# A retention layer with a Mish feed-forward on one core: a weight cast shared by two engines, GpSimd's casts ahead of a load, a state product put later, and a PSUM tile from another pool

## The chip, the cores and the metric

The kernel runs on one core of a Trainium2 chip. The core's engines run side by side: TensorE (PE) multiplies matrices, VectorE (DVE), ScalarE (ACT) and GpSimd (POOL) work elementwise, SyncE (SP) issues DMAs, and GpSimd and ScalarE can issue DMAs too. The metric is the device time of one execution in microseconds, as the median of several runs. Lower is better.

## The reference

For each batch and head a state of 64 x 64 is decayed and updated token by token; the query reads it. The result, laid out as 3072 tokens of 512 features, goes through two matrix products with an activation between them.

```python
batch, n_heads, seq, head_dim = (4, 8, 768, 64)      # q, k, v; float32
gamma = 1.0 - 2.0 ** (-5.0 - np.arange(H))
for t in range(S):
    state = gamma * state + einsum('bhd,bhe->bhde', k[:, :, t], v[:, :, t])
    y[:, :, t] = einsum('bhd,bhde->bhe', q[:, :, t], state) / sqrt(64)
x = y.transpose(0, 2, 1, 3).reshape(3072, 512)
h = x @ w_in                                          # 512 x 2048
out = (h * tanh(softplus(h))) @ w_out                 # 2048 x 512, float32
```

## The kernel before

**Chunks and blocks.** The 24 chunks of 128 tokens (six in each batch) are worked through in blocks: block 0 has four chunks, blocks 1 to 10 two each. The retention is done by chunk: `scores` multiplies k and q of one chunk (into a PSUM tile `at`), `mask` makes them causal on VectorE (`am`), `y_two` gathers a block's output `y_ps` from the masked scores and the carried state, and ScalarE copies it to `xt`, the input of the feed-forward. `state_sum` and `state_decay` carry the state on; at the first chunk of a batch `state_sum` is a single product from PSUM (L467).

**The feed-forward.** Block 0 is done plainly: `g1` makes the 16 row blocks of the hidden layer (L560) with a Mish on ScalarE behind each (L576), and `first_g2` multiplies by the output weights (L1038, L1097). Each later block is two matrices of 2 x 2 parts multiplied with seven products instead of eight. `g1_seven` is the first matrix product (L685, for the two halves g = 0 and 1 of the hidden layer), with snapshots of single products (`hsnap`, L695 on ScalarE, one on VectorE at L693), additions on VectorE (`hsum`, L705) and Mish on ScalarE (L700). `seven` is the second (L798), with sums of the hidden parts `gsum` made by VectorE (L618, L619, L764, L768), snapshots (L807) and additions (L820). The differences of weights that the seven products need are made once: `wsum` (L643) and `tmat` (L595 to L598).

**Order.** The order of the instructions on each engine is the order in which the code calls them; no scheduler moves them. An engine works through its list in order and stops at an instruction whose operands or buffers are not ready, with everything that stands behind it. Work is woven in at named steps: in block 0 `plan` says what follows which row block, in later blocks `steps_of_first` (block 1) and `steps_of` (blocks 2 to 10) give lists that `step(name)` runs.

**Output weights.** They come in four slices of 4 x 512 columns. `cast_wout(s, on_act)` makes slice s float16: VectorE casts the first part (L198), ScalarE the last `on_act` of its four parts, two at a time (L200). Slice 1 was cast whole by VectorE, behind the sums `g_sum(1)` and `g_sum(2)`. In `first_g2` the products stand in the order slice 0, the sum with `tmat`, slice 1, slice 2, and so on; between them chunk 5 (counted from 1; index CPB = 4) and the next are turned on TensorE (`turn`, L427 and L429).

**GpSimd.** It casts q (`cast_q`, L376) and v (`cast_v`, L393) and issues the DMAs of k (`bring_k`, L388, two for each chunk from the seventh on; L385 before). `gate` is a copy of one column (L401) that makes GpSimd wait for a VectorE result, here for a `tmat`. From the seventh chunk on SyncE turns q and k by DMA (`turn_by_dma`, L405), once k has landed and q is cast.

**PSUM.** Two pools share it: `mmps` with four tiles (tag `mm`) for products, `atps` with two larger tiles (tag `at`) for scores, outputs `y_ps`, states and half of the `h_ps` tiles. A tile taken from a pool waits for the last reader of the tile whose place it takes.

Of the kernel before, what the change touches and what calls it, by code (L numbers as in the profile page):

```python
# [10 lines left out]
FP32 = mybir.dt.float32  # L11
# [5 lines left out]
def kernel(  # L17
# [11 lines left out]
    d_model, d_ff = moe_w_in.shape  # L29
    P = 128  # L30
# [5 lines left out]
    CPB = TB // C  # L36
# [62 lines left out]
    for c in range(2):  # L99
        t = tri_first[c * HB:(c + 1) * HB]  # L100
# [272 lines left out]
    def cast_q(g):  # L373
        if g < NCK:
            f = qs.rearrange("p (x j) -> p x j", x=2).unsqueeze(3)
            nc.gpsimd.tensor_tensor(  # L376
                by_head(g, room16(g)[0]), by_head(0, loaded[g][0]),
                f.broadcast_to((P, 2, HP, D)), op=ALU.mult)

    def bring_k(g):  # L380
        if g < NCK:
            b, c = divmod(g, NCH)
            src = k[b, :, c * C:(c + 1) * C].rearrange("h p d -> p h d")
            if g < NCH:
                nc.gpsimd.dma_start(room16(g)[1], src)  # L385
                return
            for x in range(2):
                nc.gpsimd.dma_start(  # L388
                    room16(g)[1][:, x::2], src[:, HP * x:HP * x + HP])
# [13 lines left out]
    def turn_by_dma(g):  # L403
        qkt = qktp.tile([P, H, C], FP16, name="qkt", bufs=4)
        nc.sync.dma_start_transpose(qkt, cast[g][3].rearrange("p a h d -> p (a h d)"))  # L405
        qkts[g] = (qkt[:, :HP], qkt[:, HP:])
# [243 lines left out]
    def x_sums(blk):  # L650
# [5 lines left out]
        nc.vector.tensor_tensor(t[:, 2], b[1][1], b[0][1], op=sub)  # L656
        nc.vector.tensor_tensor(t[:, 3], b[1][0], t[:, 1], op=sub)

    def g1_seven(blk, steps):
        n = NBP // 2  # L660
        gt = gtiles[blk, 0] = gp.tile([P, NFB, 2 * P], FP16, name="g", tag="g")
        for fb in range(NFB):
            gts[blk, fb] = gt[:, fb]
        both = atps.tile([P, 2, FPS, P], FP32, name="h_ps", tag="at")
        pb, px, pe, px1 = [
            mmps.tile([P, FPS, P], FP32, name="h_ps", tag="mm") for _ in range(4)]
        pb, px, pe = [pb, both[:, 0]], [px, px1], [pe, both[:, 1]]
        m1, m5, u2 = {}, {}, {}

        def w(i, j):  # L670
            return lambda g, f, d: win(g + 2 * i, f, j * n + d)

        def s(i):
            return lambda g, f, d: wsums[g][i - 1][:, d, f * P:(f + 1) * P]

        def x(i, j):
            return lambda d: x_part(blk, i, j)[:, d]

        def t(i):
            return lambda d: tsums[blk][:, i - 1, d]  # L680

        def mm(h_ps, g, w, x, first=False):
            for f in range(FPS):
                for d in range(n):
                    nc.tensor.matmul(  # L685
                        h_ps[g][:, f], w(g, f, d), x(d), start=first and f == 0 and d == 0,
                        stop=d == n - 1, skip_group_check=True)

        def snap(h_ps, by_vector=False):
            x = hsnaps[0][:, nsnap[0] % 4].rearrange("p (f t) -> p f t", t=P)  # L690
            nsnap[0] += 1
            if by_vector:
                nc.vector.tensor_copy(x, h_ps)  # L693
            else:
                nc.scalar.copy(x, h_ps)  # L695
            return x

        def mish_of(g, i, j, h):
            fb = (g + 2 * i) * FPS
            nc.scalar.activation(  # L700
                gt[:, fb:fb + FPS, j * P:(j + 1) * P], h, AF.Mish, scale=inv_boost3)

        def plus(h_ps, x):
            h = hp.tile([P, FPS, P], FP32, name="hsum", tag="hsum", bufs=3)
            nc.vector.tensor_tensor(h, h_ps, x, op=ALU.add)  # L705
# [6 lines left out]
        def first_two(g):  # L712
            mm(px, g, w(0, 0), x(0, 0), True)
            m1[g] = snap(px[g])
            mm(pb, g, w(0, 1), x(1, 0), True)

        def second(g):
            mm(px, g, s(2), t(2))
            u2[g] = snap(px[g])

        def fifth(g):
            mm(pe, g, s(1), t(1), True)
            m5[g] = snap(pe[g], g == 0)

        first_two(0)
        step("g1")
        c0 = plus(pb[0], m1[0])
        first_two(1)
        mish_of(0, 0, 0, c0)
        step("g2")  # L730
        c1 = plus(pb[1], m1[1])
        second(0)
        mish_of(1, 0, 0, c1)
        fifth(0)
        step("g3")
        second(1)
        fifth(1)
        mm(px, 0, s(3), t(3))
        c22 = plus(px[0], m5[0])
        mm(pe, 0, s(4), x(1, 1))  # L740
        c12 = plus(pe[0], u2[0])
        mish_of(0, 1, 1, c22)
        mish_of(0, 0, 1, c12)
        step("g4")
        mm(px, 1, s(3), t(3))
        c22 = plus(px[1], m5[1])
        mm(pe, 1, s(4), x(1, 1))
        c12 = plus(pe[1], u2[1])
        mish_of(1, 1, 1, c22)
        mish_of(1, 0, 1, c12)  # L750
        step("g5")
        mm(px, 0, w(1, 1), t(4))
        mish_of(0, 1, 0, px[0])
        step("g6")

        def rest():
            mm(px, 1, w(1, 1), t(4))
            mish_of(1, 1, 0, px[1])

        return rest  # L760

    def sums_b(blk):
        (_, _, s3, _), a11, _, a21, _ = sum_views(blk)
# [6 lines left out]
    def seven(blk, steps, last, rest):  # L770
# [122 lines left out]
    def first_block():  # L893
# [81 lines left out]
        def more_sums():  # L975
# [37 lines left out]
    def first_g2():  # L1013
# [135 lines left out]
    def steps_of(blk):  # L1149
        a, nb = first[blk] + 4, blk + 1  # L1150
        if nb == len(BLOCKS):
            only, then = lambda *work: [], lambda *work: []
        else:
            only = lambda *work: list(work)
            then = only if a < NCK else lambda *work: []
        A, B = slice(0, FPS), slice(FPS, 2 * FPS)
        return {
            "g1": [*then((gate_x, blk), (cast_q, a)), (sum_next, a - 3), (decay_next, a - 3),
                   (cast_v, a), (bring_k, a + 1)],
            "g2": [(store_due, 1), (turn_and_load, a)],  # L1160
            "g3": [(store_due, 2), (sum_next, a - 2)],
            "g5": [(store_due, 3), (sums_a, blk, A)],
            "g7": [(sums_a, blk, B)],
            "m1": only((scores, a - 2), (scores, a - 1), (mask, a - 2)),
            "m5": [(sums_b, blk), *only((gate_g, blk), (decay_next, a - 2))],
            "m6": [*only((mask, a - 1)), (sums_c, blk), *then((gate_s, blk)),
                   (cast_q, a + 1), (cast_v, a + 1), (bring_k, a + 2)],
            "m2": [(turn_and_load, a + 1)],
            "m7": only((y_two, nb)),
            "m3": only((x_sums, nb)),  # L1170
        }

    def steps_of_first(blk):
        a, nb = first[blk] + 4, blk + 1
        A, B = slice(0, FPS), slice(FPS, 2 * FPS)
        return {
            "g1": [(last_ended.pop(),), (gate_x, blk), (cast_q, a - 1), (bring_k, a), (sum_next, a - 2)],
            "g2": [(turn_by_dma, a - 1), (load_v, a), (load_to, a + 2), (cast_v, a - 1), (bring_k, a + 1)],
            "g5": [(store, 2), (sums_a, blk, A)],
            "g7": [(sums_a, blk, B), (gate, gsums[1][:, 1, 2 * FPS - 1, :1]),  # L1180
                    (cast_q, a), (turn_by_dma, a), (load_q, a + 2)],
            "m1": [(scores, a - 2), (scores, a - 1), (mask, a - 2)],
            "m5": [(sums_b, blk), (gate_g, blk), (cast_v, a), ],
            "m6": [(mask, a - 1), (sums_c, blk)],
            "m2": [(gate_s, blk), (cast_q, a + 1), (cast_v, a + 1), (bring_k, a + 2),
                   (turn_by_dma, a + 1), (load_v, a + 2), (store, 2), (load_to, a + 4)],
            "m7": [(y_two, nb)],
            "m3": [(x_sums, nb)],
        }
# [38 lines left out]
```

## Time and profile before

| what | value |
|---|---|
| median of 3 runs | 197.25 us (197.18 to 197.56) |
| the profiled execution's own time | 197.34 us |
| its span in the profile | 195.3 us, 6554 instructions |
| busy: TensorE, VectorE, ScalarE, GpSimd | 187.2, 162.8, 118.7, 92.0 us |
| DMA | 36.10 MB, mean 185 GB/s |

Rows of the profile read like this. A row of the timeline has the start and length in us, engine, line, operation, what is written <- what is read, the shape, how many such instructions are merged, and in brackets how long the engine stood idle just before and what ended that. The last matmul's end is modelled, so the length of a row of matmuls has some tenths of a microsecond beyond the next row's start. A row of the waits has the engine and line that waited, the engine and line that ended it, the total in us, how often, and the longest. A row of a stage has its start and end, its length, then the busy time and number of instructions of PE, PEld (weight loads), DVE, ACT and POOL, then TensorE's granted clock, the DMA share and GB/s.

### The profile page before, as it was taken

To read this page: it belongs to the slowest core of one execution; us is meant where nothing else is said; L and a number is where in the kernel's file an instruction comes from. 1 tells how busy PE (TensorE), PEld (TensorE's weight loads), DVE (VectorE), ACT (ScalarE), POOL (GpSimd) and SP (SyncE) were. 2 spreads that over 40 slices of the span, in tenths; PEclk is the share of its full clock that TensorE was granted. 3 is DMA by queue.
4 is the path that set the end of the run, shared out by engine and by line. 5 is a ranking of instruction groups with operands and counts; after the bars stand their busy time and mean duration, and the time that the engine had idled before them with its cause. 6 is when DMAs were issued, how large, how long until landed. Compare 5 with 4: busy or idle time off the path is not lost.

```text
span 195.3 us, 6554 instructions
## 1 busy us (share of the span) xinstructions
PE 187.2 (96%) x2722; PEld 158.1 (81%) x2722; DVE 162.8 (83%) x329; ACT 118.7 (61%) x216; POOL 92.0 (47%) x135
## 2 busy tenths in 40 slices
PE   6999999899999999999999999999999999999982
PEld 2557645786788998988988988988988988989982
DVE  3688699979989898897897897897897997897861
ACT  3364797263693693693782782882873963954950
POOL 4270205497466954935915917907807814010000
PEclk9999999999999999999999999999999999999999
DMA  5999999996699999996995995993996983202003
GB/s 173 350 373 405 405 408 234 303 227 44 107 188 246 143 315 185 186 205 166 158 190 142 184 168 154 189 229 91 197 146 165 194 131 94 76 0 86 25 3 107
DMA packets 95805, 36.10 MB, mean 185 GB/s; under 512 B 82592, under 2 KB 89376, under 8 KB 95776
## 3 DMA queue, kind: packets, MB, share of 16 engines
q1 hardware_dynamic: 74544, 33.04, 65.1%
q0 software_dynamic: 21088, 2.62, 23.8%
q8 instruction: 21, 0.34, 0.7%
q14 instruction: 8, 0.07, 0.1%
q10 hardware_dynamic: 144, 0.03, 0.1%
HBM read 27.30 MB, written 6.29 MB: 172 GB/s over the span
## 4 chain that ended last, share of the span: by engine, by line
PE 80%; DVE 13%; ACT 3%; issue 2%; POOL 0%; POOLq 0%; DVEq 0%
PE o_ps L798 31%; PE h_ps L685 30%; PE o_ps L1038 4%; PE at L443 3%; DVE wsum L643 3%; PE y_ps L512 3%; PE at L419 2%; PE h_ps L889 2%; ACT g L700 1%; PE y_ps L503 1%; DVE am L449 1%; DVE wout L198 1%; DVE hsum L705 1%; DVE am L295 1%; PE u_ps L458 1%
## 5 line engine op out<-in xcount | busy, mean ns | idle before, releaser
L705 DVE TENSOR_TENSOR hsum<-h_ps,hsnap 128x512 f32<-128x512 f32 x60 | 38.5, 685 | 5.9 <-PE h_ps L685 3.3
L700 ACT ACTIVATE g<-hsum 128x512 f16<-128x512 f32 x60 | 36.9, 630 | 3.7 <-DVE hsum L705 3.6
L695 ACT COPY hsnap<-h_ps 128x512 f32<-128x512 f32 x50 | 28.0, 582 | 14.6 <-PE h_ps L685 14.6
L685 PEld LDWEIGHTS <-wsum 128*128 128x128 f16 x640 | 36.3, 98 | 0.5 <-issue 0.3
L798 PEld LDWEIGHTS <-gsum 128*128 128x128 f16 x336 | 30.4, 98 | 4.6 <-issue 0.7
L685 PE MATMUL h_ps<-xsum,wsum 128*128 128x128 f16 x480 | 30.4, 219 | 0.1
L798 PE MATMUL o_ps<-tmat,gsum 128*128 128x256 f16 (+1 forms) x256 | 29.5, 266 | 0.7 <-ACT g L700 0.7
L685 PEld LDWEIGHTS <-win 128*128 128x128 f16 x480 | 28.2, 98 | 1.8 <-issue 0.4
L388 POOL DMA_DIRECT2D qk<-in_k_dram x36 | 27.8, 776 | 0.0
L401 POOL COPY gate<-gsum 128x1 f16<-128x1 f16 x18 | 3.4, 186 | 49.9 <-DVE gsum L764 39.1
L545 ACT CAST xt<-y_ps 128x1024 f16<-128x1024 f32 x10 | 10.1, 1012 | 25.2 <-PE y_ps L503 22.2
L798 PEld LDWEIGHTS <-g 128*128 128x128 f16 x256 | 23.4, 98 | 2.4
L449 DVE TENSOR_TENSOR am<-at,tri 128x1024 f16<-128x1024 f32 x20 | 24.3, 1218 | 0.5 <-PE at L443 0.5
L393 POOL TENSOR_TENSOR v<-vf,qvs 128x512 f16<-128x512 f32 x20 | 21.3, 1067 | 2.6 <-DMA vf<-in_v_dram 2.6
L820 DVE TENSOR_TENSOR osb<-o_ps,snap 128x256 f32<-128x256 f32 (+1 forms) x31 | 12.0, 411 | 11.9 <-ACT xt L545 9.9
L376 POOL TENSOR_TENSOR qk<-qf,qvs 128x512 f16<-128x512 f32 x20 | 21.9, 1093 | 0.0
L798 PE MATMUL o_ps<-wout,g 128*128 128x256 f16 (+1 forms) x168 | 20.8, 267 | 0.0
L685 PE MATMUL h_ps<-xt,win 128*128 128x128 f16 x320 | 19.7, 219 | 0.3 <-ACT osb L1108 0.3
L807 ACT COPY snap<-o_ps 128x256 f32<-128x256 f32 (+1 forms) x32 | 11.3, 357 | 6.9 <-PE o_ps L798 6.8
L685 PE MATMUL h_ps<-xsum,win 128*128 128x128 f16 x160 | 12.3, 220 | 0.0
L685 PE MATMUL h_ps<-xt,wsum 128*128 128x128 f16 x160 | 12.2, 219 | 0.0
L700 ACT ACTIVATE g<-h_ps 128x512 f16<-128x512 f32 x20 | 11.9, 594 | 0.0
(124 smaller groups left out, 283.9 us busy)
## 6 DMA issues: line engine op xcount, KB each, us to landing
vf<-in_v_dram SPq DMA_DIRECT2D x24, 256.0 KB, 5.3
out_dram<-osb SPq DMA_DIRECT2D x22, 256.0 KB, 4.7
qf<-in_q_dram SPq DMA_DIRECT2D x20, 256.0 KB, 4.3
wi<-in_moe_w_in_dram SPq DMA_DIRECT2D x3, 1024.0 KB, 10.7
wt<-in_moe_w_out_dram SPq DMA_DIRECT2D x3, 1024.0 KB, 8.8
qk<-in_k_dram POOLq DMA_DIRECT2D x36, 64.0 KB, 4.1
qfirst<-in_q_dram SPq DMA_DIRECT2D x2, 512.0 KB, 4.3
kf<-in_k_dram SPq DMA_DIRECT2D x4, 256.0 KB, 4.9
```

Source lines behind the costliest of these rows:

```text
L376: nc.gpsimd.tensor_tensor(by_head(g, room16(g)[0]), by_head(0, loaded[g][0]), f.broadcast_to((P, 2, HP, D)), op=ALU.mult)
L388: nc.gpsimd.dma_start(room16(g)[1][:, x::2], src[:, HP * x:HP * x + HP])
L393: nc.gpsimd.tensor_tensor(room16(g)[2], loaded[g][2], vs.unsqueeze(2).broadcast_to((P, H, D)), op=ALU.mult)
L449: nc.vector.tensor_tensor(am, ats.pop(g), tri.unsqueeze(1).unsqueeze(1).broadcast_to((P, 2, HP, C)), op=ALU.mult)
L545: nc.scalar.copy(xts[blk][:, :, :2 * C], y_ps.rearrange("p i j c -> p i (j c)"))
L685: nc.tensor.matmul(h_ps[g][:, f], w(g, f, d), x(d), start=first and f == 0 and d == 0, stop=d == n - 1, skip_group_check=True)
L695: nc.scalar.copy(x, h_ps)
L700: nc.scalar.activation(gt[:, fb:fb + FPS, j * P:(j + 1) * P], h, AF.Mish, scale=inv_boost3)
L705: nc.vector.tensor_tensor(h, h_ps, x, op=ALU.add)
L798: nc.tensor.matmul(t, x(f), w(f)[:, c], start=first and f == 0, stop=f == n - 1, skip_group_check=True)
L807: nc.scalar.copy(x[:, c], t)
L820: nc.vector.tensor_tensor(dst[:, c], t, plus[:, c], op=ALU.add)
```

## The change

Four things change in what the engines do:

1. **Slice 1 of the output weights.** `cast_wout(1)` becomes `cast_wout(1, 2)`: VectorE casts two parts of four, ScalarE the other two. It is called one row block later in `plan` (13 instead of 12), and ahead of `g_sum(2)` and `g_sum(3)`. On VectorE it now stands directly behind `g_sum(1)`, on ScalarE between the Mish of the 13th and of the 14th row block.
2. **The eighth chunk's k.** In `first_g2`, `bring_k(CPB + 3)` with its two DMAs moves behind `cast_v(CPB + 1)`, `cast_v(CPB + 2)` and `cast_q(CPB + 2)` in GpSimd's list. SyncE's list keeps its order.
3. **A state product.** In block 1 `sum_next(a - 2)` moves from the step behind the second product to the step behind the fourth `hsum` (`at4`): L467 stands three rows of `hsum` and a snapshot later in VectorE's list.
4. **The last block's second matrix product.** `pe` and `pb` become the two halves of one `at` tile instead of two `mm` tiles.

`g1_seven` is also rewritten: the order that its calls had is now a text, `ORDER`, whose words name works (`first.0`, `c11.0`, `g11.0`) and steps (`at1` to `at6`, before `g1` to `g6`). The order itself is the same.

```diff
+    ORDER = """
+        first.0 second.0 at1 c11.0 first.1 second.1 g11.0 at2 c11.1 sixth.0 g11.1 fifth.0 at3
+        sixth.1 fifth.1 seventh.0 c22.0 third.0 c12.0 g22.0 g12.0 at4
+        seventh.1 c22.1 third.1 c12.1 g22.1 g12.1 at5 fourth.0 at6"""
...
+        @does("first")
+        def _(g):
+            mm(px, g, w(0, 0), x(0, 0), True)
+            m1[g] = snap(px[g])
...
@@ seven
-        pe = mmps.tile([P, hf], FP32, name="o_ps", tag="mm")
+        if last:
+            pe = atps.tile([P, 2, d_model], FP32, name="o_ps", tag="at")
+            pb, pe = pe[:, 0, :hf], pe[:, 1, :hf]
+        else:
+            pe = mmps.tile([P, hf], FP32, name="o_ps", tag="mm")
...
-        pb = mmps.tile([P, hf], FP32, name="o_ps", tag="mm")
+        if not last:
+            pb = mmps.tile([P, hf], FP32, name="o_ps", tag="mm")
@@ first_block
-                12: [(g_sum, 1), (g_sum, 2), (cast_wout, 1), (room_for_more,), (g_sum, 3)],
+                12: [(g_sum, 1)],
+                13: [(cast_wout, 1, 2), (room_for_more,), (g_sum, 2), (g_sum, 3)],
@@ first_g2
         bring_k(CPB + 2)
-        bring_k(CPB + 3)
         cast_v(CPB + 1)
...
         cast_v(CPB + 2)
         cast_q(CPB + 2)
+        bring_k(CPB + 3)
         turn_by_dma(CPB + 2)
@@ steps_of_first
-            "g1": [(last_ended.pop(),), (gate_x, blk), (cast_q, a - 1), (bring_k, a), (sum_next, a - 2)],
+            "at1": [(last_ended.pop(),), (gate_x, blk), (cast_q, a - 1), (bring_k, a)],
...
+            "at4": [(sum_next, a - 2)],
```

More of the change, by code (lines that the diff above doesn't have):

```diff
@@ L710, in step, with does, note, _ @@
                 fn(*args)
-        def first_two(g):
+        pluses, works = {}, {}
+        def does(name):
+            def note(fn):
+                works[name] = fn
+            return note
+        @does("first")
+        def _(g):
             mm(px, g, w(0, 0), x(0, 0), True)
             m1[g] = snap(px[g])
+        @does("second")
+        def _(g):
             mm(pb, g, w(0, 1), x(1, 0), True)
-        def second(g):
+        @does("sixth")
+        def _(g):
             mm(px, g, s(2), t(2))
@@ L719, in second, with _ @@
             u2[g] = snap(px[g])
-        def fifth(g):
+        @does("fifth")
+        def _(g):
             mm(pe, g, s(1), t(1), True)
             m5[g] = snap(pe[g], g == 0)
[L725 to L758, printed above, removed]
@@ L760, in g1_seven, with _ @@
-        return rest
+        @does("seventh")
+        def _(g):
+            mm(px, g, s(3), t(3))
+        @does("third")
+        def _(g):
+            mm(pe, g, s(4), x(1, 1))
+        @does("fourth")
+        def _(g):
+            mm(px, g, w(1, 1), t(4))
+            mish_of(g, 1, 0, px[g])
+        @does("c11")
+        def _(g):
+            pluses[g, 0, 0] = plus(pb[g], m1[g])
+        @does("c22")
+        def _(g):
+            pluses[g, 1, 1] = plus(px[g], m5[g])
+        @does("c12")
@@ new lines, in _, with do @@
+        def _(g):
+            pluses[g, 0, 1] = plus(pe[g], u2[g])
+        @does("g11")
+        def _(g):
+            mish_of(g, 0, 0, pluses[g, 0, 0])
+        @does("g22")
+        def _(g):
+            mish_of(g, 1, 1, pluses[g, 1, 1])
+        @does("g12")
+        def _(g):
+            mish_of(g, 0, 1, pluses[g, 0, 1])
+        def do(order):
+            for word in order.split():
+                name, _, g = word.partition(".")
+                if name in works:
+                    works[name](int(g))
+                else:
+                    step(name)
@@ L762, in sums_b @@
+        do(ORDER)
+        return lambda: do("fourth.1")
     def sums_b(blk):
@@ L774, in seven @@
         px = [mmps.tile([P, wide], FP32, name="o_ps", tag="mm") for _ in range(parts)]
-        pe = mmps.tile([P, hf], FP32, name="o_ps", tag="mm")
+        if last:
+            pe = atps.tile([P, 2, d_model], FP32, name="o_ps", tag="at")
+            pb, pe = pe[:, 0, :hf], pe[:, 1, :hf]
+        else:
+            pe = mmps.tile([P, hf], FP32, name="o_ps", tag="mm")
         osb = [op.tile([P, d_model], FP32, name="osb", tag="osb") for _ in range(2)]
@@ L1157, in steps_of @@
         return {
-            "g1": [*then((gate_x, blk), (cast_q, a)), (sum_next, a - 3), (decay_next, a - 3),
+            "at1": [*then((gate_x, blk), (cast_q, a)), (sum_next, a - 3), (decay_next, a - 3),
                    (cast_v, a), (bring_k, a + 1)],
-            "g2": [(store_due, 1), (turn_and_load, a)],
-            "g3": [(store_due, 2), (sum_next, a - 2)],
-            "g5": [(store_due, 3), (sums_a, blk, A)],
+            "at2": [(store_due, 1), (turn_and_load, a)],
+            "at3": [(store_due, 2), (sum_next, a - 2)],
+            "at5": [(store_due, 3), (sums_a, blk, A)],
             "g7": [(sums_a, blk, B)],
@@ L1176, in steps_of_first @@
         return {
-            "g1": [(last_ended.pop(),), (gate_x, blk), (cast_q, a - 1), (bring_k, a), (sum_next, a - 2)],
-            "g2": [(turn_by_dma, a - 1), (load_v, a), (load_to, a + 2), (cast_v, a - 1), (bring_k, a + 1)],
-            "g5": [(store, 2), (sums_a, blk, A)],
+            "at1": [(last_ended.pop(),), (gate_x, blk), (cast_q, a - 1), (bring_k, a)],
+            "at2": [(turn_by_dma, a - 1), (load_v, a), (load_to, a + 2), (cast_v, a - 1), (bring_k, a + 1)],
+            "at4": [(sum_next, a - 2)],
+            "at5": [(store, 2), (sums_a, blk, A)],
             "g7": [(sums_a, blk, B), (gate, gsums[1][:, 1, 2 * FPS - 1, :1]),
```

## The prediction

> **What bounds the kernel now.** I read the engine totals first, then what TensorE waited for, then its busy time stage by stage.
>
> ```profile
> PE 187.2 (96%) x2722; PEld 158.1 (81%) x2722; DVE 162.8 (83%) x329; ACT 118.7 (61%) x216; POOL 92.0 (47%) x135
> ```
> ```profile
> PE o_ps L1038 <- DVE wout L198: 0.8, 1, 0.8
> PE o_ps L798 <- ACT g L700: 0.7, 1, 0.7
> PE h_ps L685 <- ACT osb L1108: 0.3, 1, 0.3
> ```
> ```profile
> 34.82:49.48 14.66, 14.66 (x168) 11.04 (x169) 13.09 (x17) 6.20 (x8) 10.92 (x11) 1.00 0.97 189
> 49.48:56.34 6.86, 6.43 (x106) 6.00 (x105) 6.07 (x15) 5.26 (x11) 4.76 (x7) 1.00 0.85 120
> 64.72:70.52 5.80, 5.80 (x106) 5.80 (x104) 5.36 (x13) 4.57 (x9) 3.28 (x6) 1.00 1.92 194
> ```
>
> TensorE is busy 96% of the span at the full granted clock (1.00 in each stage), so only its few waits can be won. There are three places: 0.8 us for output slice 1's cast, 0.7 us in the last block, and the first product of block 1, which takes 6.86 us where the same 104 matmuls take 5.80 us one block later. That is 1.06 us lost in short waits, of which the row of 0.3 us is the largest. The change touches all three places. The rewriting of `g1_seven` as a list of words leaves each engine's instructions in the order they had, so it costs nothing; in blocks 2 to 9 nothing changes.
>
> **Slice 1's cast.** Rows by engine: TensorE, VectorE, ScalarE, GpSimd.
>
> ```profile
> 32.95 1.05 PE L1038 MATMUL o_ps<-tmat,gsum 128*128 128x256 f16 x8
> 34.82 3.67 PE L1038 MATMUL o_ps<-wout,g 128*128 128x256 f16 x32 [0.82 <-DVE wout L198]
> 39.19 0.39 PE L427 MATMUL t_ps<-ident,qk 128*128 128x128 f16 x4
> ```
> ```profile
> 32.21 0.68 DVE L1005 TENSOR_TENSOR gsum<-g 128x1024 f16<-128x1024 f16 x1
> 33.54 1.22 DVE L198 CAST wout<-wt 128x2048 f16<-128x2048 f32 x1
> 35.28 0.69 DVE L198 CAST wout<-wt 128x1024 f16<-128x1024 f32 x1
> 36.07 0.69 DVE L596 TENSOR_TENSOR tmat<-wout,tmat 128x1024 f16<-128x1024 f16 x1
> ```
> ```profile
> 29.64 0.60 ACT L576 ACTIVATE g<-h_ps 128x512 f16<-128x512 f32 x1 [0.27 <-PE h_ps L560]
> 32.23 0.60 ACT L576 ACTIVATE g<-h_ps 128x512 f16<-128x512 f32 x1 [0.27 <-PE h_ps L560]
> 34.30 1.05 ACT L200 CAST wout<-wt 128x1024 f16<-128x1024 f32 x1
> ```
> ```profile
> 28.99 0.35 POOL L401 CAST gate<-wt 128x1 f16<-128x1 f32 x1 [5.17 <-DMA wt<-in_moe_w_out_dram]
> 37.37 1.50 POOL L376 TENSOR_TENSOR qk<-qf,qvs 128x512 f16<-128x512 f32 x1
> ```
>
> Thirty-two matmuls in a row take 3.67 us and eight take 1.05, so one more costs 2.62 / 24 = 0.109 us, and eight back to back 0.87. The group at 32.95 would be followed at 33.82; it is followed at 34.82, when the cast of 1.22 us that began at 33.54 is over. That stall is 1.0 us.
>
> After the change VectorE casts half, right behind the sum at 32.21. It begins at about 32.89, takes 0.69 (the row at 35.28 is such a half) and is over at 33.58, 0.24 us ahead of need. ScalarE casts the other half behind the activation that ends at 30.24, until about 31.29 (1.05, as in the row at 34.30). The data has landed: GpSimd's copy at 28.99 waited for that same slice. Queued behind this new instruction are three activations. The first two move by up to 0.8 us, but the last starts at 32.23 as TensorE lets it, so the backlog is gone before the copies that follow, and the first two PSUM tiles are written again only by the groups behind that last activation's own matmuls. It costs nothing. If the ScalarE cast took twice as long, the last activation would slip by some 0.5 us, and by the same the fourth group of four matmuls.
>
> Behind the cast, VectorE has 1.22 − 0.69 = 0.53 us less to do, and the second sum no longer waits 0.1 us for the first; so `tmat` at 36.07 comes 0.6 us sooner. GpSimd's gate waits for that `tmat`, so the q cast behind it (37.37 to 38.87) ends at 38.27. TensorE wants that q at 39.19 − 1.0 = 38.19, so 0.1 us of the 1.0 becomes a wait for GpSimd. **Net 0.9 us**, with 0.7 and 1.0 as bounds.
>
> **The middle: does VectorE keep up until block 1 ends?** Between 39 and 49 us TensorE runs without a gap, so its 0.9 us reaches block 1 unless VectorE or GpSimd hold it back.
>
> ```profile
> 41.26 3.05 POOL L388 DMA_DIRECT2D qk<-in_k_dram x4
> 46.30 1.53 POOL L376 TENSOR_TENSOR qk<-qf,qvs 128x512 f16<-128x512 f32 x1
> ```
> ```profile
> 46.85 1.52 DVE L597 TENSOR_TENSOR tmat<-wout,wout 128x1024 f16<-128x1024 f16 x1
> 51.36 0.42 DVE L1106 TENSOR_TENSOR osb<-o_ps,osb 128x256 f32<-128x256 f32 x1
> 51.70 0.41 DVE L467 TENSOR_TENSOR stc<-u_ps,gcv 128x256 f16<-128x256 f32 x1
> 52.03 1.28 DVE L705 TENSOR_TENSOR hsum<-h_ps,hsnap 128x512 f32<-128x512 f32 x2
> 54.66 2.48 DVE L705 TENSOR_TENSOR hsum<-h_ps,hsnap 128x512 f32<-128x512 f32 x4 [0.76 <-PE h_ps L685]
> ```
> ```profile
> 57.31 0.62 PE L443 MATMUL at<-qkt 64*128 64x128 f16 x16
> ```
> ```profile
> 50.22 0.59 ACT L695 COPY hsnap<-h_ps 128x512 f32<-128x512 f32 x1
> 50.69 0.39 ACT L1108 COPY osb<-o_ps 128x256 f32<-128x256 f32 x1
> ```
>
> GpSimd issues four k DMAs at 41.26 (3.05 us) and only then does three casts. The change leaves two DMAs (1.53 us) ahead of them and puts the eighth chunk's two behind. The last cast, 46.30 to 47.83 now, begins 0.6 + 1.53 us sooner, near 44.2, and stands beside VectorE's masks instead of beside `tmat` at 46.85. That row took 1.52 us; the like one at 36.07, with no cast beside it, took 0.69. So VectorE gains up to 0.8 us here.
>
> The Trainium skill (SBUF — State Buffer, "Who interferes with whom") says that a VectorE instruction with two SBUF inputs and a GpSimd one that reads SBUF exclude each other for a whole instruction. The trace agrees: the row at 46.85 ends at 48.37, 0.54 us after the cast's end at 47.83. By that rule the sum stands; were the 1.52 us the instruction's own, the first `hsum` would come some 0.3 us later and the total would be 195.9.
>
> With that, VectorE is no longer late by itself: block 1's first `hsum` hangs on TensorE. The first eight matmuls begin at 49.48 − 0.9 = 48.58 and need 0.45 us (eight of the 104 that take 5.80) and 0.18 more until the last result (the 1.05 − 0.87 above), until 49.2; ScalarE's snap (0.59) and copy (0.39) last until 50.2, the `osb` addition (0.42) until 50.6. The state product at 51.70, a step of 0.33 us (52.03 − 51.70), is no longer in between, so the first `hsum` starts at 50.6 instead of 52.03: 1.4 us sooner. The 0.3 us wait for L1108 goes, and the later waits shrink. I put what is left of the 1.06 us at 0.4 to 0.5, an estimate; TensorE would then leave the product 0.9 + 0.6 = 1.5 us sooner.
>
> But the state product is only put off: it now stands behind the fourth `hsum`, and VectorE works without a gap from the third (54.66) on. From the fifth on VectorE is sooner by 1.4 − 0.33 = 1.1 us, against TensorE's 1.5 us. I allow its later waits for sums 0.1 us of cover (an estimate), so by the end of block 2 TensorE is back at **1.2 us sooner**, the 0.9 included. Bounds: 0.6, if VectorE's chain shifts by no more than slice 1's 0.6 us; 1.5, if margins cover all. I take 1.2, the place of the sums that end last. The new wait of the next scores for the state product is covered: it is done by 54.7, and the scores at 57.31 are due 1.5 us sooner, at 55.8.
>
> **The tail.** Rows of TensorE, ScalarE, VectorE:
>
> ```profile
> 185.08 0.61 PE L685 MATMUL h_ps<-xsum,win 128*128 128x128 f16 x8
> 186.34 1.93 PE L798 MATMUL o_ps<-tmat,gsum 128*128 128x256 f16 x24 [0.65 <-ACT g L700]
> ```
> ```profile
> 185.71 0.58 ACT L700 ACTIVATE g<-h_ps 128x512 f16<-128x512 f32 x1
> 186.49 0.62 ACT L700 ACTIVATE g<-h_ps 128x512 f16<-128x512 f32 x1
> 187.41 0.71 ACT L807 COPY snap<-o_ps 128x256 f32<-128x256 f32 x2 [0.30 <-PE o_ps L798]
> ```
> ```profile
> 185.05 0.42 DVE L618 TENSOR_TENSOR gsum<-g 128x512 f16<-128x512 f16 x1
> 185.85 0.42 DVE L618 TENSOR_TENSOR gsum<-g 128x512 f16<-128x512 f16 x1
> ```
>
> The group at 186.34 waits for the activation that ends at 186.29, the last reader of its PSUM bank. On the scores' banks that wait goes; next late is its operand, in halves: the first sum is there at 185.47, the second at 186.27. Matmuls 1 to 4 run while the second is awaited and 5 to 8 at 186.32, so the group ends four matmuls sooner: 4 × 0.109 = **0.44 us**. The shared tile adds two waits. The product after next (due at 186.76 + 0.89 = 187.65) now waits for this group's snap, which follows the activation at 186.49: 187.11 + 0.37 (half of the row at 187.41) = 187.48. Two products on, due near 189.4, the pass that adds to this tile waits for the first addition, which follows the matmuls that end near 188.7 and takes 0.4: 189.1. Both are covered, by 0.2 and 0.3 us. Behind the waiting TensorE everything that is left would queue; with one cover gone the gain falls to 0.2.
>
> **Sum.** 1.2 + 0.44 = 1.64 us off the profiled execution's own 197.34 us gives 195.7. The median of the runs before, 197.25, lies 0.09 lower, so I predict **195.6 us**.
>
> **Rivals.** (1) VectorE and GpSimd keep the middle: the casts moved now stand beside VectorE's smaller works (state, slice 1's `tmat`), its chain comes only 0.6 us sooner, and the result is 197.25 − 0.6 − 0.44 = 196.2. For it speaks that VectorE is busy 13.09 of 14.66 us there; against it that its longest rows are long only beside a cast. Chance 0.14.
>
> (2) The tail gives nothing, because the sum at 186.27 ends 0.02 us before the activation, and TensorE waits for all of it: 197.25 − 1.2 = 196.0. Against it: the halves are awaited apart. Chance 0.08.
>
> (3) Slower: the eighth chunk's k is late.
>
> ```profile
> 52.78 1.24 SPq L405 DMA_TRANSPOSE qkt<-qk x1
> qkt<-qk SPq DMA_TRANSPOSE x2, 3.5
> DMA to landing us min/median/max: 2.9/4.1/5.9
> ```
>
> The last row is that of the k DMAs. The eighth chunk's pair now issues behind the last cast, at 44.2 + 1.53 = 45.7 and 46.5 at the latest, instead of 42.8 and 43.5. SyncE turns that chunk once its q cast is done, at 52.78 − 1.4 = 51.4, and the turn lands 3.5 us later, at 54.9; the scores need it at 55.9. With the longest landing, 5.9 us, k is there at 52.4, the turn lands at 55.9 and nothing is lost. From a landing of 7.6 us on, the stall eats the whole gain; at 9 us it is 3.1 us and the time 198.7. [...] Chance 0.05.
>
> (4) The first gain is swallowed whole by the wait for GpSimd's q and v, and only the tail counts: 196.8. Chance 0.03.
>
> **Numbers.** The forecast has 0.70. Its own range, from bounds of 0.9 to 1.5 and 0.38 to 0.45, is 195.3 to 196.0; with (1), (2) and the unknown sizes I give 195.1 to 196.4. The difference that a measurement of this kernel can tell is about 0.2%, 0.4 us. All cases lie below 196.86 but (3), and what of (4) is worse than its price: faster 0.92, same 0.03, slower 0.05.
>
> **What would show it.** Right: the group behind 32.95 follows at 33.8 without a wait for L198; the transposes at about 38.3 wait shortly for GpSimd; block 1's first product takes 6.2 to 6.4 us; L597 beside no cast takes 0.7; in the last block the eight matmuls split four and four around the second sum. Wrong: a new wait of TensorE over 0.3 us between 36 and 62 us, most likely for DVE hsum or POOL qk; block 1's product still at 6.8; or a wait of scores for the transposed qkt.

## The result, and the profile after

The changed kernel takes 195.5 us (median of four runs, 195.40 to 196.03) against 197.2 us before; the ratio is 0.9915 with an interval of 0.9893 to 0.9936. Six more runs, beside the experiments, gave 195.9 us and 0.9932 (0.9913 to 0.9951). The profiled execution took 195.58 us, its span 193.6.

The engine totals, and then every wait of TensorE of 0.2 us or more (line waited at, what released it; us in all, times, longest):

```profile
PE 186.7 (96%) x2722; PEld 157.6 (81%) x2722; DVE 162.0 (84%) x329; ACT 119.5 (62%) x217; POOL 91.5 (47%) x135
```
```profile
PE at L419 <- POOL tri L93: 1.9, 1, 1.9
PE t_ps L270 <- ACT qk L256: 0.5, 1, 0.5
PE at L288 <- DVE am L295: 0.2, 1, 0.2
PE o_ps L830 <- DVE gsum L618: 0.2, 1, 0.2
PE o_ps L1072 <- DVE gsum L1039: 0.2, 1, 0.2
```

The three waits that the prediction named (0.8 for slice 1's cast, 0.7 in the last block, 0.3 for `osb`) are gone. The first three waits above belong to the start, which the change does not touch; the fourth is the tail's second sum, and the fifth stands ahead of slice 1 (see the last section). With the same 2722 matmuls TensorE's busy time is 0.5 us less than before and its idle time 1.2 us less (6.9 against 8.1). The two cannot be parted sharply, since a matmul that is held up for a moment can count as busy: before, 6.43 of the 6.86 us of block 1's first product were busy, with matmuls that take 5.80 one block later.

TensorE, VectorE, ScalarE and GpSimd around slice 1 (start, duration; L1038 of before is now L1072, L1005 is L1039):

```profile
32.89 1.05 PE L1072 MATMUL o_ps<-tmat,gsum 128*128 128x256 f16 x8 [0.17 <-DVE gsum L1039]
33.77 3.66 PE L1072 MATMUL o_ps<-wout,g 128*128 128x256 f16 x32
38.20 0.40 PE L427 MATMUL t_ps<-ident,qk 128*128 128x128 f16 x4
```
```profile
32.75 0.69 DVE L198 CAST wout<-wt 128x1024 f16<-128x1024 f32 x1
35.35 0.69 DVE L596 TENSOR_TENSOR tmat<-wout,tmat 128x1024 f16<-128x1024 f16 x1
```
```profile
29.79 1.04 ACT L200 CAST wout<-wt 128x1024 f16<-128x1024 f32 x1
30.73 1.76 ACT L576 ACTIVATE g<-h_ps 128x512 f16<-128x512 f32 x3
```
```profile
36.65 1.50 POOL L376 TENSOR_TENSOR qk<-qf,qvs 128x512 f16<-128x512 f32 x1
```

The slice's group follows the group ahead of it 0.88 us later (32.89 to 33.77), where it was 1.87 us (32.95 to 34.82): 0.99 us won. VectorE's half is over at 33.44. ScalarE works off its three activations without a gap, so the new cast costs nothing there. From slice 1's group to the first transpose it is 4.43 us instead of 4.37: 0.06 us went into the wait for GpSimd's q.

VectorE, GpSimd and TensorE from 44 us to the end of block 1's first product (L705 is now L709, L685 L689, L798 L830):

```profile
45.70 0.68 DVE L597 TENSOR_TENSOR tmat<-wout,wout 128x1024 f16<-128x1024 f16 x1
50.44 1.28 DVE L709 TENSOR_TENSOR hsum<-h_ps,hsnap 128x512 f32<-128x512 f32 x2
53.07 1.29 DVE L709 TENSOR_TENSOR hsum<-h_ps,hsnap 128x512 f32<-128x512 f32 x2 [0.76 <-PE h_ps L689]
54.28 0.42 DVE L467 TENSOR_TENSOR stc<-u_ps,gcv 128x256 f16<-128x256 f32 x1
54.61 1.28 DVE L709 TENSOR_TENSOR hsum<-h_ps,hsnap 128x512 f32<-128x512 f32 x2
```
```profile
44.20 1.03 POOL L376 TENSOR_TENSOR qk<-qf,qvs 128x512 f16<-128x512 f32 x1
45.18 1.55 POOL L388 DMA_DIRECT2D qk<-in_k_dram  x2
```
```profile
48.50 1.95 PE L689 MATMUL h_ps<-xt,win 128*128 128x128 f16 x32
54.76 1.04 PE L830 MATMUL o_ps<-wout,g 128*128 128x256 f16 x8
```

GpSimd's last cast comes 2.1 us sooner, L597 takes 0.68 us instead of 1.52, and the first `hsum` starts 1.59 us sooner. The product takes 6.26 us (48.50 to 54.76) instead of 6.86, so TensorE leaves it 1.58 us sooner. The fifth `hsum` (54.61) stands behind the state product.

Rows of the chain of work that ended last show what that costs one block later: start, duration and matmuls of the first products of blocks 1 and 2, and then block 2's of the kernel before.

```profile
48.66 6.25 PE h_ps L689 x104
63.35 6.04 PE h_ps L689 x104
```
```profile
64.88 5.81 PE h_ps L685 x104
```

Some 0.23 us are given back there, and the last block's first matmuls start 1.31 us sooner than before (first row: before; second: changed).

```profile
178.38 1.95 PE L685 MATMUL h_ps<-xt,win 128*128 128x128 f16 x32
```
```profile
177.07 1.95 PE L689 MATMUL h_ps<-xt,win 128*128 128x128 f16 x32
```

The tail, and then the last group of the kernel before:

```profile
183.78 0.61 PE L689 MATMUL h_ps<-xsum,win 128*128 128x128 f16 x8
184.23 0.61 PE L830 MATMUL o_ps<-tmat,gsum 128*128 128x256 f16 x4
185.02 1.50 PE L830 MATMUL o_ps<-tmat,gsum 128*128 128x256 f16 x20 [0.19 <-DVE gsum L618]
189.00 1.06 PE L830 MATMUL o_ps<-tmat,g 128*128 128x128 f16 x16
```
```profile
190.74 1.06 PE L798 MATMUL o_ps<-tmat,g 128*128 128x128 f16 x16
```

The eight matmuls split four and four around the second sum. From the changed kernel's first row to its last group it is 5.22 us, against 5.66 before (185.08 to 190.74): 0.44 us.

### The profile page after: what moved, and what is told of

Same layout as the page of the kernel before. It is cut to its first block, busy times and chain, and to the rows that moved or that the text cites. A ratio compares the mean times of both kernels' runs of the same rounds, so it can differ in the third digit from the quotient of the medians.

```text
span 193.6 us, 6554 instructions
## 1 busy us (share of the span) xinstructions
PE 186.7 (96%) x2722; PEld 157.6 (81%) x2722; DVE 162.0 (84%) x329; ACT 119.5 (62%) x217; POOL 91.5 (47%) x135
## 4 chain that ended last, share of the span: by engine, by line
PE 85%; DVE 8%; issue 2%; ACT 1%; POOL 0%; POOLq 0%; DVEq 0%
PE h_ps L689 32%; PE o_ps L830 32%; PE o_ps L1072 5%; PE y_ps L512 3%; PE at L443 3%; DVE wsum L643 3%; PE at L419 2%; PE o_ps L1131 2%; PE h_ps L922 2%; PE y_ps L503 1%; DVE am L295 1%; PE u_ps L458 1%; DVE win L190 1%; DVE hsum L709 1%; DVE wout L198 1%
## 5 line engine op out<-in xcount | busy, mean ns | idle before, releaser
L709 DVE TENSOR_TENSOR hsum<-h_ps,hsnap 128x512 f32<-128x512 f32 x60 | 38.5, 685 | 6.0 <-PE h_ps L689 3.7
L689 PEld LDWEIGHTS <-wsum 128*128 128x128 f16 x640 | 36.4, 98 | 0.4
L830 PEld LDWEIGHTS <-gsum 128*128 128x128 f16 x336 | 30.3, 98 | 4.4 <-DVE gsum L618 0.5
L689 PE MATMUL h_ps<-xsum,wsum 128*128 128x128 f16 x480 | 30.4, 219 | 0.0
L830 PE MATMUL o_ps<-tmat,gsum 128*128 128x256 f16 (+1 forms) x256 | 29.7, 266 | 0.2 <-DVE gsum L618 0.2
L689 PEld LDWEIGHTS <-win 128*128 128x128 f16 x480 | 28.1, 98 | 1.4
L830 PEld LDWEIGHTS <-g 128*128 128x128 f16 x256 | 23.4, 98 | 2.3
L376 POOL TENSOR_TENSOR qk<-qf,qvs 128x512 f16<-128x512 f32 x20 | 21.4, 1068 | 0.0
L830 PE MATMUL o_ps<-wout,g 128*128 128x256 f16 (+1 forms) x168 | 20.8, 267 | 0.0
L689 PE MATMUL h_ps<-xt,win 128*128 128x128 f16 x320 | 19.5, 219 | 0.0
L689 PE MATMUL h_ps<-xsum,win 128*128 128x128 f16 x160 | 12.3, 220 | 0.0
L689 PE MATMUL h_ps<-xt,wsum 128*128 128x128 f16 x160 | 12.2, 219 | 0.0
```

Of the source, the lines that this page charges most:

```text
L376: nc.gpsimd.tensor_tensor(by_head(g, room16(g)[0]), by_head(0, loaded[g][0]), f.broadcast_to((P, 2, HP, D)), op=ALU.mult)
L689: nc.tensor.matmul(h_ps[g][:, f], w(g, f, d), x(d), start=first and f == 0 and d == 0, stop=d == n - 1, skip_group_check=True)
L830: nc.tensor.matmul(t, x(f), w(f)[:, c], start=first and f == 0, stop=f == n - 1, skip_group_check=True)
```

## The experiments

Profiles of single executions differ by up to 0.9 us ahead of slice 1's group, where nothing is changed. So the stages behind it are compared, by the starts of TensorE's groups. S: from the eight matmuls ahead of slice 1's group to that group. T: from there to the first transpose. P1, P2: the first products of blocks 1 and 2. E: from the last block's last first-product group to its last group. All in us; the ratio is to the kernel before.

| kernel | S | T | P1 | P2 | E | median | ratio and interval |
|---|---|---|---|---|---|---|---|
| before | 1.87 | 4.37 | 6.86 | 5.81 | 5.66 | 197.2 to 197.3 | |
| changed | 0.88 | 4.43 | 6.26 | 6.04 | 5.22 | 195.5 | 0.9915 (0.9893 to 0.9936) |
| changed_again | 0.88 | 4.43 | 6.25 | 6.03 | 5.22 | 195.88 | 0.9932 (0.9913 to 0.9951) |
| slice1_alone | 0.88 | 4.43 | 7.11 | 5.81 | 5.67 | 196.69 | 0.9972 (0.9957 to 0.9987) |
| tail_alone | 1.87 | 4.37 | 6.86 | 5.81 | 5.23 | 196.83 | 0.9972 (0.9958 to 0.9985) |
| slice1_back | 1.86 | 4.38 | 6.25 | 6.04 | 5.23 | 196.99 | 0.9979 (0.9964 to 0.9994) |
| slice1_whole | 1.14 | 4.70 | 6.26 | 6.26 | 5.23 | 196.13 | 0.9948 (0.9929 to 0.9966) |
| slice1_behind | 1.33 | 4.38 | 6.26 | 6.40 | 5.23 | 195.92 | 0.9930 (0.9910 to 0.9949) |
| k_back | 0.89 | 4.43 | 6.79 | 6.04 | 5.23 | 196.31 | 0.9953 (0.9935 to 0.9970) |
| state_back | 0.89 | 4.42 | 6.59 | 5.81 | 5.23 | 195.75 | 0.9931 (0.9912 to 0.9949) |
| state_third | 0.89 | 4.42 | 6.25 | 5.81 | 5.23 | 195.56 | 0.9903 (0.9878 to 0.9928) |
| k_mid | 0.89 | 4.43 | 6.26 | 6.04 | 5.23 | 195.58 | 0.9919 (0.9899 to 0.9939) |
| k_mid_third | 0.89 | 4.42 | 6.26 | 5.81 | 5.22 | 195.31 | 0.9899 (0.9883 to 0.9915) |
| k_late | 0.89 | 4.43 | 6.26 | 5.81 | 5.22 | 199.49 | 1.0111 (1.0087 to 1.0135) |

**The parts alone.** On the kernel before:

```diff
-                12: [(g_sum, 1), (g_sum, 2), (cast_wout, 1), (room_for_more,), (g_sum, 3)],
+                12: [(g_sum, 1)],
+                13: [(cast_wout, 1, 2), (room_for_more,), (g_sum, 2), (g_sum, 3)],
```

> The kernel before, with only the cast of output slice 1 halved and moved ahead of the second sum. Theory of the prediction: TensorE reaches block 1 some 0.9 us sooner, but the eighth chunk's k still holds up GpSimd, L597 stays at about 1.5 us beside its last cast, and the state product still stands ahead of the first hsum; so VectorE's chain, only 0.6 us sooner, takes part of it back and the time falls by 0.6 to 0.7 us, to about 196.55. Rival (slice 1 is all, the moved k and state product do nothing): the whole gain ahead of the tail is here, 1.3 us, 195.95. Rival (swallowed by the wait for GpSimd's q): 197.1.

Measured: 196.69 us. Slice 1's gain is there in full (S), and block 1's product takes 0.25 us more than before, 7.11: VectorE is not ready for a TensorE that comes sooner, so 0.99 − 0.06 − 0.25 = 0.68 us are left by the profile (0.60 by the medians). Both rivals, 195.95 and 197.1, lie outside the interval (196.4 to 197.0). Then the tail's tile alone, also on the kernel before:

```diff
-        pe = mmps.tile([P, hf], FP32, name="o_ps", tag="mm")
+        if last:
+            pe = atps.tile([P, 2, d_model], FP32, name="o_ps", tag="at")
+            pb, pe = pe[:, 0, :hf], pe[:, 1, :hf]
+        else:
+            pe = mmps.tile([P, hf], FP32, name="o_ps", tag="mm")
...
-        pb = mmps.tile([P, hf], FP32, name="o_ps", tag="mm")
+        if not last:
+            pb = mmps.tile([P, hf], FP32, name="o_ps", tag="mm")
```

> The kernel before, with only the last block's first and second operand products (pb, pe) on one tile of scores' banks. Theory: the eight matmuls that waited 0.65 us for an activation now split four and four around the second sum, 4 x 0.109 = 0.44 us less: 196.8. Rival (the wait for the whole sum takes the wait's place): 197.2. Rival (the shared tile's new waits show): 197.0.

Measured: 196.83 us, and E falls by 0.43 us. That speaks against both rivals: neither a wait for the whole sum nor the waits on the shared tile show in it.

**Slice 1 in the changed kernel.** Taken back whole:

```diff
-                12: [(g_sum, 1)],
-                13: [(cast_wout, 1, 2), (room_for_more,), (g_sum, 2), (g_sum, 3)],
+                12: [(g_sum, 1), (g_sum, 2), (cast_wout, 1), (room_for_more,), (g_sum, 3)],
```

> The changed kernel with slice 1 cast whole by VectorE behind the second sum, as before; the moved k, the moved state product and the tail stay. Prediction's price for slice 1, 0.9 us, of which the rest of the middle took back nothing: 196.4. Rival (VectorE's chain sets the middle, and it comes only 0.6 us later): 196.1. Rival (the k that is issued last sets it, which does not depend on slice 1's cast but on VectorE's tmat): 195.8.

Measured: 196.99 us; by the ratios, 0.9979 against 0.9932 on the same chip, slice 1 is worth 0.47% or 0.93 us here, with P1 and P2 unchanged. The median is 0.6 us above the number expected; 0.4 of that is in the level of these runs, in which the changed kernel has 195.88 instead of 195.5. Raised by as much, the rivals would stand at 196.5 and 196.2, below the interval (196.6 to 197.2).

Then its two halves apart: whole, but ahead of the second sum; and halved, but behind it.

```diff
-                13: [(cast_wout, 1, 2), (room_for_more,), (g_sum, 2), (g_sum, 3)],
+                13: [(cast_wout, 1), (room_for_more,), (g_sum, 2), (g_sum, 3)],
```

> The changed kernel with slice 1 ahead of the second sum, but cast whole by VectorE. Theory: the cast takes 1.22 instead of 0.69 us, ends 0.2 to 0.3 us behind TensorE's need (32.75 + 1.22 = 33.97 against 33.77), and the tmat behind it comes 0.5 us later, so GpSimd's q makes TensorE wait 0.5 us more at the transposes: 195.9 to 196.2. Rival (the order is all of the gain, the halving none): 195.6.

```diff
-                13: [(cast_wout, 1, 2), (room_for_more,), (g_sum, 2), (g_sum, 3)],
+                13: [(g_sum, 2), (cast_wout, 1, 2), (room_for_more,), (g_sum, 3)],
```

> The changed kernel with slice 1 cast in halves by two engines, but VectorE's half behind the second sum. Theory: it ends 0.6 us later, at 34.04 against 33.77, so TensorE waits 0.3 us; the tmat comes no later, and nothing else moves: 195.9. Rival (the halving is all of the gain, the order none): 195.6.

Measured: 196.13 and 195.92 us, both where the theory has them. But the medians alone show nothing here: the changed kernel's own were 195.5 and 195.88, and the intervals of the ratios overlap. What shows it is the stages. Cast whole, the slice costs 0.26 us at its group (S) and 0.27 us at the transposes (T), since `tmat` and GpSimd's q come later. Cast in halves behind the sum, it costs 0.45 us at its group and wins back 0.05 at the transposes. So of the 0.93 us the order alone brings some 0.4, the halving alone some 0.5. In these two profiles, each of the longest run of its kernel, P2 also took 0.2 to 0.4 us more than in the changed kernel. There GpSimd's q cast (L376) waits 1.2 us for the load of its q, the product behind it (L475) comes as late, and VectorE's L470 waits for that (1.17 and 1.21 us) ahead of the third `hsum`. Whether the edits make that load late is open.

**The eighth chunk's k.** Back ahead of the casts:

```diff
         bring_k(CPB + 2)
+        bring_k(CPB + 3)
         cast_v(CPB + 1)
...
-        bring_k(CPB + 3)
```

> The changed kernel, with the eighth chunk's k issued ahead of the casts again, as before. Theory: GpSimd's last cast comes 1.5 us later and stands beside L597, which takes about 1.5 instead of 0.68 us; the first hsum comes some 0.8 us later; block 1's first product takes 6.6 to 6.8 us instead of 6.26, and by the end 0.3 to 0.6 us are lost: 195.8 to 196.1. Rival (TensorE, not VectorE's L597, sets the first hsum, and later cover absorbs the rest): 195.5, no difference.

Measured: 196.31 us, 0.2 us above the range, and the rival's 195.5 lies below the interval (196.0 to 196.7). Of this kernel, VectorE and GpSimd:

```profile
46.70 1.52 DVE L597 TENSOR_TENSOR tmat<-wout,wout 128x1024 f16<-128x1024 f16 x1
51.54 1.28 DVE L709 TENSOR_TENSOR hsum<-h_ps,hsnap 128x512 f32<-128x512 f32 x2
```
```profile
46.15 1.52 POOL L376 TENSOR_TENSOR qk<-qf,qvs 128x512 f16<-128x512 f32 x1
```

L597 is at 1.52 us again. It ends at 48.22, 0.55 us behind the cast beside it (47.67), as it did before (0.54 us). Measured from block 1's start (49.06 here, 48.50 in the changed kernel), the first `hsum` is 0.54 us later, and P1 0.53 us longer. So L597's time is the cast's doing, and it reaches TensorE.

**The state product.** Back ahead of the first `hsum`:

```diff
-            "at1": [(last_ended.pop(),), (gate_x, blk), (cast_q, a - 1), (bring_k, a)],
+            "at1": [(last_ended.pop(),), (gate_x, blk), (cast_q, a - 1), (bring_k, a), (sum_next, a - 2)],
...
-            "at4": [(sum_next, a - 2)],
```

> The changed kernel with the state product L467 back ahead of the first hsum. The prediction's reason: its step of 0.33 us delays the first hsum and with it the product, TensorE leaves it up to 0.3 us later, 195.8. Rival (from the changed kernel's trace: VectorE idles 0.76 us ahead of the third step's hsum, so a delay of 0.33 us ahead of it is absorbed, and L467 no longer stands behind the fourth): 195.2 to 195.5.

Measured: 195.75 us, beside 195.88 of the changed kernel on the same chip: no difference. Each theory is right in one part. The delay is not absorbed in block 1, as the prediction has it and the rival does not; in block 2 time comes back, as the rival has it. TensorE's row of this kernel has the new wait:

```profile
52.31 1.21 PE L689 MATMUL h_ps<-xsum,wsum 128*128 128x128 f16 x16 [0.31 <-DVE hsum L709]
```

P1 is 0.33 us longer, and P2 0.22 us shorter, because L467 no longer stands in the gapless row of sums behind the fourth. So the move from one place to the other is worth about nothing. There is a third place, where VectorE idles 0.76 us ahead of the third `hsum`:

```diff
-            "at4": [(sum_next, a - 2)],
+            "at3": [(sum_next, a - 2)],
```

> The changed kernel, with the state product L467 moved from behind the fourth hsum to behind the third step, where the profile shows VectorE idle for 0.76 us (ahead of the hsum at 53.07). Theory: what TensorE lost between block 1's first product (1.58 us sooner than before) and the last block (1.31 us sooner) is the state product's 0.33 us step on VectorE's gapless chain; in the idle time it costs nothing, so the time falls by up to 0.27 us, to 195.2 to 195.3. Rival (the lead is lost to ScalarE or to GpSimd's casts beside VectorE): 195.5, no difference. Rival (it delays the hsum behind it): 195.7.

Measured: 195.56 us (195.06 to 196.45), above the 195.2 to 195.3 expected; the median cannot tell it from the first rival's 195.5, but the stages can. Both products are at their best (P1 6.25, P2 5.81). The profiled execution lost that and more in a wait that of the other profiles only k_late's has, further below:

```profile
56.85 0.40 PE L443 MATMUL at<-qkt 64*128 64x128 f16 x8 [0.82 <-DMA qkt<-qk]
```
That is the eighth chunk. The landing of the four k DMAs from 40 to 47 us, the last two the eighth chunk's, in state_third, in the changed kernel and in the kernel before:

```profile
DMA to landing us min/median/max: 3.1/4.4/5.5
```
```profile
DMA to landing us min/median/max: 3.0/3.5/5.1
```
```profile
DMA to landing us min/median/max: 2.9/3.0/3.4
```

GpSimd's cast of that chunk's q, and SyncE's transpose, in state_third and then in the changed kernel:

```profile
50.08 1.04 POOL L376 TENSOR_TENSOR qk<-qf,qvs 128x512 f16<-128x512 f32 x1
51.52 1.24 SPq L405 DMA_TRANSPOSE qkt<-qk  x1
```
```profile
50.16 1.04 POOL L376 TENSOR_TENSOR qk<-qf,qvs 128x512 f16<-128x512 f32 x1
51.24 1.25 SPq L405 DMA_TRANSPOSE qkt<-qk  x1
```

In state_third k landed at 51.4, behind the q cast (51.12). The transpose went out at 51.52 and landed 5.3 us later, at 56.8; the second eight of the scores' matmuls wanted it at 55.9. In the changed kernel k landed at 51.1, just ahead of the end of the q cast (51.20). The transpose went out at 51.24 and landed 4.2 us later, at 55.4, and was wanted at 56.0. So the cover there is 0.6 us, and of the 1.4 us that state_third's transpose landed later, 1.1 are the transpose's own time.

The place of k goes with a late landing. In the seven profiles with k at its new place the longest of the four landings is 5.0 to 5.9 us, in the six others with four of them 3.1 to 4.3. With k at the new place, the seventh chunk's transpose goes out sooner, and SyncE issues a q load of 256 KB beside the k (at 46.65 in the changed kernel, 49.95 before). That this load delays k fits, but no run tested it alone. Nothing ties the state product to these landings, and one profile cannot tell how often they come so late; to see whether the changed kernel has it too, it was run again.

> The changed kernel once more, beside three kernels of the same chip that differ from it in one place each, to have its time and its spread from more runs: 195.5. If the landing of the eighth chunk's k and of its transpose, which was 0.3 to 0.6 us ahead of its need in the changed kernel's profile, is sometimes late, single runs spread upward by up to 0.8 us; if that lateness came only with the state product moved to the third step, they lie within 0.3 us of each other.

Measured: 195.88 us, 195.49 to 196.39. Of the three upper runs the profiled one (196.09 us) is not k's doing: it has no wait for `qkt`, and its 0.5 us stand ahead of slice 1's group, which starts at 34.28 instead of 33.77. The other two have no profile.

**A place for k between.** Both kernels issue it one cast sooner; the first also has the state product in the third place.

```diff
         cast_v(CPB + 2)
+        bring_k(CPB + 3)
         cast_q(CPB + 2)
-        bring_k(CPB + 3)
```

> The changed kernel with the state product behind the third step and the eighth chunk's k one cast sooner (ahead of the sixth chunk's last q cast instead of behind it). Theory: state_third's profile lost 0.82 us of TensorE to the transposed qkt of that chunk, whose k landed last (5.5 us, after the q cast); issued 1 us sooner it lands ahead of the q cast, the stall goes, and the gapless chain behind the fourth hsum has 0.33 us less: 195.0 to 195.2. Rival (the q cast, 1.5 us later, stands beside L597 and lengthens it, as with k_back): 195.6 to 196.0.

> The changed kernel with the eighth chunk's k ahead of the sixth chunk's last q cast, the state product left behind the fourth hsum. Theory: against k_mid_third (195.31 us) it lacks the 0.25 us that the state product's place gives back in block 2's first product: 195.5 to 195.6, the changed kernel's own median, but with no run above 195.9, since k lands 1.5 us sooner and the scores never wait for its transpose. Rival (k_mid_third owed its gain to k alone): 195.3.

Measured: 195.31 us (195.08 to 195.38) and 195.58 us (195.38 to 196.21). The first is 0.1 us above what was expected and the lowest median of all: its ratio is 0.9899 (0.9883 to 0.9915) beside 0.9932 (0.9913 to 0.9951) of the changed kernel on the same chip; the interval of that kernel's first four runs (0.9893 to 0.9936) overlaps it. The second is at the expected median, 0.27 us behind the first, and P2 (6.03 against 5.81) has that difference, so the gain is not k's alone. But one run of its six is above 195.9, which was not expected; that run has no profile. The products of k_mid_third in the chain:

```profile
48.70 6.26 PE h_ps L689 x104
63.33 5.81 PE h_ps L689 x104
```

Why L597 does not suffer beside the cast that now follows k, in the rows of VectorE and GpSimd of k_mid:

```profile
45.51 0.69 DVE L597 TENSOR_TENSOR tmat<-wout,wout 128x1024 f16<-128x1024 f16 x1
```
```profile
45.76 1.32 POOL L376 TENSOR_TENSOR qk<-qf,qvs 128x512 f16<-128x512 f32 x1
```

L597 began first, and it is the cast that takes longer (1.32 against 1.03 us).

**The slower rival, made to happen.** The k behind GpSimd's wait for `xsum`:

```diff
-        bring_k(CPB + 3)
...
-            "at1": [(last_ended.pop(),), (gate_x, blk), (cast_q, a - 1), (bring_k, a)],
+            "at1": [(last_ended.pop(),), (gate_x, blk), (bring_k, a - 1), (cast_q, a - 1), (bring_k, a)],
```

> The changed kernel with the eighth chunk's k issued later still: in block 1, behind GpSimd's wait for xsum and ahead of that chunk's q cast. This prices the prediction's slower rival. Theory (k's landing and then the transpose's decide): issued near 50.2 to 51.7, landed 3 to 5 us behind (55 to 56.5), turned and landed some 4 us behind that (59 to 61), where the scores want it at 55.7: TensorE stalls 3 to 5 us, of which covers later may return up to 0.5; 198.5 to 200.5. Rival (the profile's order hides a second cover and the scores wait little): under 196.5.

Measured: 199.49 us. The mechanism is the one named, but the wait itself is smaller than expected and the loss is not. TensorE's rows, and its busy time by stretch (after the stretch: its length, then busy time of PE, PEld, DVE, ACT, POOL with the number of instructions; then the granted clock, the DMA share and GB/s):

```profile
58.10 0.40 PE L443 MATMUL at<-qkt 64*128 64x128 f16 x8 [2.20 <-DMA qkt<-qk]
58.89 3.07 PE L830 MATMUL o_ps<-tmat,gsum 128*128 128x256 f16 x16
```
```profile
55.90:58.10 2.20, 0.00 (x0) 0.00 (x0) 2.13 (x5) 1.18 (x3) 1.73 (x4) 1.00 1.61 175
58.10:59.30 1.20, 1.20 (x20) 1.06 (x21) 1.20 (x3) 0.21 (x1) 0.52 (x2) 1.00 1.51 227
59.50:62.60 3.10, 3.10 (x16) 2.19 (x15) 1.61 (x2) 0.93 (x3) 2.40 (x4) 0.50 1.21 329
62.80:64.00 1.20, 1.20 (x13) 1.01 (x10) 0.43 (x1) 0.00 (x0) 1.20 (x2) 0.97 1.15 245
```

The scores wait 2.20 us, and 1.3 us after they run again the granted clock falls to half for some 3.4 us. From block 1's second product to block 2's first it is 12.43 us (54.53 to 66.96) instead of 8.43 (54.76 to 63.19): 4.0 us, of which the wait is only 2.2.

## Why the prediction was right

By its own steps, against the profiled execution's 1.74 us (last group at 190.74, now 189.00), of which 0.06 us lie ahead of the change:

- Slice 1: the stall of 1.0 is gone (0.99), 0.1 became a wait for GpSimd's q (0.06). Net 0.9 predicted, 0.93 measured.
- L597 beside no cast: 0.7 predicted, 0.68 measured. That the 1.52 us were the cast's doing and not its own is shown by k_back and k_mid. By the Trainium skill (SBUF — State Buffer, "SBUF: two separate sides") whichever of the two starts first holds the shared ports for the whole instruction; the traces agree on which of them pays, VectorE in k_back (1.52 us) and GpSimd in k_mid (1.32 us).
- The first `hsum`: 1.4 us sooner predicted, 1.59 measured. Block 1's product won 0.6 us predicted, 0.60 measured. Of that 0.53 is k's part and 0.33 the state product's, each by undoing it alone; together they exceed 0.60, since slice 1's gain costs 0.25 us in this product when it comes alone.
- The give-back behind the fourth `hsum`: 0.3 us predicted, some 0.27 measured (1.58 to 1.31 us sooner), 0.23 of it in block 2's first product. state_third and state_back show that L467 is its cause: without it there the product takes 5.81 us.
- The tail: 0.44 us predicted, 0.44 measured, with the split of four and four.

The rivals: (1) fell by the changed kernel's own profile (L597, P1), (2) by tail_alone, (4) by slice1_alone. (3) did not happen in the changed kernel, but two of its terms were off. It let the transpose land 3.5 us after its issue, which left 1.0 us of cover (54.9 against 55.9); the transpose took 4.2 us in the changed kernel, which left 0.6, and 5.3 in state_third, where the scores waited. That the q cast is the last thing ahead of the transpose was right for the changed kernel, but by 0.1 us only, and not for state_third. And it priced a stall by its length, 198.7 us for one of 3.1; k_late had 2.2 us of stall and took 199.49, because of the clock. The chance of 0.05 stood on a cover that was thinner, and a price that was higher, than written.

That the median of the first four runs meets the 195.6 us to 0.1 is partly luck: six more runs of the same kernel gave 195.88. What the prediction had right is the steps, each within 0.2 us.

## What to carry to other kernels

Where TensorE is busy 96% of the time, follow each gain to the end: a group that comes 1 us sooner is worth that only if the engine that works beside it comes sooner too, and the price of a small instruction depends on whether it stands in a row without gaps or in front of an idle stretch, which the profile shows. Where an instruction is long only beside another engine's, look at which of the two starts first: here the later one paid. When a load is put off, measure its landing at the new place, and price the stall that it may cause with the clock that follows it.

## What the runs showed of the hardware

A pause of TensorE of 2.20 us, with full load on either side, was followed by a granted clock of 0.50 from about 59.4 to 62.8 us, which cost 1.8 us more. That is k_late's one profile, but its other runs agree: the mean granted clock of all four is 0.987 to 0.991, that of every other run here at least 0.996. The pause of 0.82 us in state_third had no such effect: its clock stayed at 1.00 in the next 5 us. The Trainium skill (TensorE: Matmul & The Clock Gate, "Why this matters for your kernels") advises against pauses of more than about 3 us; here one of 2.2 us was enough.

GpSimd's pair of DMA issues at the start (L385) and VectorE's cast of slice 0 (L198, 2048 elements) overlap, and their durations come in three pairs over the 14 profiles: 2.6 to 2.8 us with a cast of 1.22 us (seven), 2.58 with 1.50 (five), 1.97 with 1.62 (two). Where the cast is longer, the sum behind it makes TensorE wait 0.17 to 0.28 us, as at 32.89 in the changed kernel, and not otherwise. That one of the two waits for the other fits, but no run tested it.
